# Four of sixteen first-norm transposes moved from TensorE to SBUF-to-SBUF transfers, with a new order of all tasks, in a gated convolution and mixer kernel

## The chip, the core and the metric

The kernel runs on one core of one Trainium2 chip. A core has five engines with queues of their own: TensorE (PE in the profile, with its weight loads as PEld), VectorE (DVE), ScalarE (ACT), GpSimd (POOL) and SyncE (SP), which here mainly issues transfers; sixteen DMA engines move the data. The metric is the device time of one execution in microseconds (us), lower is better.

## The reference, cut to what matters

There are 2048 tokens of 640 channels. Everything is bfloat16 at the borders.

```python
x = A_q
g = sigmoid((x * gate_w).sum(-1, keepdims=True))
# A: a 4-tap causal filter of k times v, then a convolution over all 2048 tokens, times q
kv = shift4(k, shift_k) * v
y  = irfft(rfft(pad(kv)) * rfft(pad(ssm_k)))[:2048] + kv * ssm_D
a  = x * y
# B: a mixer block on the same x
h  = gelu(layernorm(x) @ w1)                  # 640 -> 640
hs = concat(four quarters of h, shifted by +1, -1, +2, -2 tokens) @ w2
x1 = x + hs
b  = x1 + gelu(layernorm(x1) @ w3) @ w4       # 640 -> 1536 -> 640
out = g * a + (1 - g) * b
```

## The kernel before, in words

**Layout.** Token 16·p + s sits on partition p in slot s, so x is 16 slots of 128 tokens by 640 channels. A matmul that contracts over channels needs the normalised rows the other way round, channels on partitions; that turning is what the change is about.

**Branch B.** For each slot s, `st1.s` takes mean and variance (on DVE by batch-norm instructions, L577 to L581, or on ACT by two passes with an accumulator, L585 and L586), `rs1.s` makes the reciprocal root on POOL (L595), and `nm1.s` writes the normalised row into one of four `xn` buffers (DVE L631, ACT L601). For each pair of slots `tr1.s` turns both rows by 2 x 5 TensorE transposes of 128x128 into PSUM (L609), and `ev1.s` copies them into `xnT` (ACT L387 or DVE L389). `w1.G.part` (L689, and L693 for part 4) multiplies four slots of group G by w1; the token shifts are in the choice of slots that it reads, so group 3 with a shift of 2 reads slots 10 to 13. `g1` is the GELU (ACT L706), `w2.s` the second matmul (L715), `x1.s` the residual sum (DVE L722), `sq.s` the sum of squares (ACT L727). The second norm is done in the same way (`ve2`, `st2` on POOL, `nm2`), but its rows are turned by `dt2.s`, a transposing transfer from SBUF to SBUF that SP issues (L808), into `x1nT` or, for groups 1 and 3, into `XB`. `w3.c.fb` (L817) with `g2` (L824), and `w4.s` (L833, L842) follow.

**Branch A.** `ldsk` loads the filter; `trh` turns it on TensorE (L859), `evt` evicts it, `dfold` adds ssm_D on POOL (L865). `kv` is 32 passes on DVE (L878, L882, L886). The long convolution is a two-stage Fourier transform by matmuls: `s1h` (L911) and `s1x` (L913) with evictions `e1h` and `e1x` into the two `FS` buffers, `wF` to DRAM (L943), `rF` back (L957), `s2h` and `s2x` (L965), products `pa` and `pb` (DVE L980), `s3` (L993), `wG` (L1005), `rG` (L1019), `s4` (L1031). The end is `yq` (L1037), `ad` (L1064) or `ax` (L1045), `fo` (L1051) for the four last slots, and the stores `st`. `ldq` loads q again for `yq`.

**Order.** Each step is a task with a number; there are 778. `ORDER` is a list of these numbers, with a letter where a task that can run on several engines has its engine set. Each engine runs its own tasks in the order of the list, so a task that waits holds up all that stands behind it on that engine. `Plan.place` (L147) walks the list with a table of estimated durations and picks buffers by it: eight PSUM banks ("U", taken singly or as an aligned pair), four `xn`, two `FS` and so on. It also decides how many filler matmuls (L255) go in front of a TensorE task. Fillers are only put in until `w1.1.2` runs, which gives up the bank that they write. The 16 transposed rows of the first norm all go over TensorE, since the tuple that selects pairs for the transfers is empty:

```python
    DMA1 = ()
    pairs = [2, 4, 6, 8, 0, 14, 10, 12]
```

Of the kernel before, what the change touches and what calls it, by code (L numbers as in the profile page):

```python
# [42 lines left out]
163 406 130 128 156 157 440 105a 441a 407 159 153 154 106 160 461 47 445a 402 131 158 109a 155 442 111 132 137 443a
112a 408 161 462 466 48 138 409 463a 448 134 135 468 215p 216 449 164 140 469a 467a 119 413 141 51 221p 165 470 410 50
411 120a 166 222 223v 464 465a 167 474 471a 173 475a 174 171 217a 480 168 476 187 191 481a 482 193 477a 172 473 192
188 412 414 218 483a 478 169 195 189 170 181 415 416 417 479a 472 418 419 421 422 182 178 179 485 196 194 190 486 423
488 219a 484 225a 489a 175 220 487a 492 176 493a 136 203 424 204 494 425 490 206 498 207 495a 200 201 491a 420 426 427
428 430 502 499a 226 177 504 224 505a 211 503a 506 500 227 496 501a 239 507a 133 497 228 240 508 142 429 184 185 139
247 431 432 433 434 435 436 248 233 510 512 511a 231 513a 243 259p 509 249 514 235 234 260 232 244 515a 518 245 265p
250 236 229 52 519a 516 437 212 246 517a 520 241 242 237 230 522 266 261v 523v 526 238 530 527a 197 524 531a 528 255  # L50
521 529a 269v 262 525v 186 694v 263a 180 205 208 532 267v 303v 198 253 251 257 256 533 183 268 309v 353v 213 202 310
254 270 252 304 313a 264 307v 199 311v 534 535 537 271 539 258 536v 305a 538a 354 540 541v 272 571 566 542 555 293 544
543a 545 572 294 574 575a 289 567 569 570v 573a 550 290 277 598 556 558 278 568v 291 551 557a 292 552a 306 559v 553
546 554a 547a 279 280 283 576 577 284 548v 603 604 606 607a 599 587 287 635 312 273 600a 288 560 561 562 274 285 564a
605v 601 355v 308 286 563v 588 589a 590 591a 602v 582 275 276 578 314 614 580a 619 608 583 609 347p 348 579a 315 325
316 667 584v 549 585 357v 586a 214 615 617 335 616v 620 326 622 336 623a 592 618a 317 323 318 324 621v 593 610 611a
630 612v 333 636 334 631 633 329 349v 662 319 637v 624 634a 646 706 632a 625 594 281 330 320 647 595a 596v 648v 724
# [1049 lines left out]
```

## Time and profile before

| | us |
|---|---|
| device time, median of 3 runs (lowest, highest) | 225.08 (224.55, 225.7) |
| the profiled execution, its own time | 227.05 |
| its span, first to last instruction | 225.3 |
| TensorE busy (94%) | 212.7 |
| VectorE busy (84%) | 189.3 |
| ScalarE busy (69%) | 154.4 |
| GpSimd busy (20%) | 45.8 |

The profiled execution lies 1.75 us above its span and about 2 us above the median. In a row of a timeline the columns are start, duration, engine, line, operation, output and inputs, how many instructions are merged, and in brackets the idle time before with what ended it. In a row of grouped instructions they are line, engine, operation, count, then total busy time and mean duration in ns, then idle time before. In the table of stretches each row is a stretch of the span with its length, the busy time and count of each engine, the granted TensorE clock, the share of the DMA engines in use and their rate. "Median us to landing" is from issue to the last byte's arrival.

### The profile page before, as it was taken

The numbers are of one execution on the slowest core, as the hardware profiler recorded it, in microseconds if no ns is written. First come the engines' busy times: TensorE is split into PE (matmuls) and PEld (weight loads), VectorE is DVE, ScalarE is ACT, GpSimd is POOL, SyncE is SP. The second block draws the span as 40 slices with busy tenths as digits, with TensorE's granted clock in tenths as the row PEclk, the third lists the DMA queues.
The fourth block names the chain that finished last, engine by engine and source line by source line (L and its number), as shares of the span: only waits on it lengthen the run. The fifth ranks groups of instructions, "written<-read, shape, count | busy, mean of one in ns | idle before, by whom it ended". The sixth has DMA issues, their size and how long they took to land.

```text
span 225.3 us, 5381 instructions
## 1 busy us (share of the span) xinstructions
PE 212.7 (94%) x2161; PEld 106.4 (47%) x2178; DVE 189.3 (84%) x281; ACT 154.4 (69%) x225; POOL 45.8 (20%) x86
## 2 busy tenths in 40 slices
PE   3999889899999999999999999999999999999992
PEld 1576454466444444345543433334444555555561
DVE  7998896999999999997469989899857426989984
ACT  6998969799988999889658988888675002225000
POOL 7481532436200009930710000000000000000000
PEclk9999999999999999999999999999999999999999
DMA  6999999999999998979899989999992596988624
GB/s 193 281 308 232 220 237 238 327 233 327 349 240 287 241 272 252 379 270 270 193 367 311 373 154 285 316 304 309 247 255 88 185 374 209 281 250 249 203 64 116
DMA packets 39503, 57.94 MB, mean 257 GB/s; under 512 B 15027, under 2 KB 30645, under 8 KB 39478
## 3 DMA queue, kind: packets, MB, share of 16 engines
q1 hardware_dynamic: 39158, 57.27, 89.9%
q10 hardware_dynamic: 320, 0.33, 0.5%
q8 instruction: 17, 0.28, 0.5%
q14 instruction: 8, 0.07, 0.1%
HBM read 35.56 MB, written 18.36 MB: 239 GB/s over the span
## 4 chain that ended last, share of the span: by engine, by line
PE 63%; DMA 17%; DVE 12%; SPq 3%; issue 2%; ACT 1%; DVEq 0%
PE PS L817 18%; PE PS L833 17%; PE PS L715 9%; DMA x<-in_A_q_dram 7%; PE PS L965 5%; DMA W<-in_B_w_dram 4%; PE PS L689 4%; PE PS L993 4%; DMA SK<-in_A_ssm_k_dram 3%; DVE VC L878 3%; DVE VC L882 3%; DMA QO<-in_A_q_dram 2%; SPq L382 2%; PE PS L911 2%; PE PS L1031 1%
## 5 line engine op out<-in xcount | busy, mean ns | idle before, releaser
L824 ACT ACTIVATE h2T<-PS 128x512 bf16<-128x512 f32 x48 | 27.9, 605 | 27.3 <-PE PS L817 26.9
L833 PE MATMUL PS<-W,h2T 128*128 128x512 bf16 (+3 forms) x306 | 39.8, 298 | 0.3
L387 ACT CAST FS<-PS 128x1024 bf16<-128x1024 f32 x37 | 36.0, 1021 | 5.4 <-PE PS L913 3.5
L817 PEld LDWEIGHTS <-W 128*128 128x128 bf16 (+1 forms) x300 | 22.1, 103 | 29.4 <-issue 8.4
L833 PEld LDWEIGHTS <-h2T 128*128 128x128 bf16 (+1 forms) x312 | 22.4, 100 | 18.5 <-issue 1.6
L387 ACT CAST XH<-PS 128x1024 bf16<-128x1024 f32 x26 | 25.5, 1020 | 7.5 <-PE PS L965 7.4
L817 PE MATMUL PS<-x1nT,W 128*128 128x512 bf16 x120 | 28.5, 380 | 0.0
L817 PE MATMUL PS<-XB,W 128*64 128x512 bf16 (+1 forms) x180 | 28.5, 380 | 0.0
L980 DVE TENSOR_TENSOR PP<-XH 128x2048 bf16<-128x2048 bf16 x20 | 23.6, 1219 | 3.1 <-ACT XH L387 2.8
L878 DVE TENSOR_TENSOR VC<-K,VC 128x2560 bf16<-128x2560 bf16 x16 | 23.7, 1490 | 2.3 <-DMA W<-in_B_w_dram 2.1
L715 PE MATMUL PS<-W,hsT 128*128 128x128 bf16 (+1 forms) x155 | 23.5, 297 | 0.9 <-DMA W<-in_B_w_dram 0.6
L850 DVE TENSOR_TENSOR x<-PS,x 128x640 bf16<-128x640 f32 x12 | 9.8, 823 | 13.4 <-PE PS L833 13.2
L689 PE MATMUL PS<-xnT,W 128*128 128x512 bf16 x80 | 19.2, 379 | 0.1
L715 PEld LDWEIGHTS <-hsT 128*128 128x128 bf16 x160 | 12.8, 98 | 13.0 <-issue 1.1
L882 DVE TENSOR_TENSOR VC<-VC 128x2560 bf16<-128x2560 bf16 x12 | 17.9, 1489 | 0.3
L389 DVE CAST XH<-PS 128x1024 bf16<-128x1024 f32 x14 | 16.9, 1220 | 1.2 <-PE PS L965 1.1
L1037 DVE SCALAR_TENSOR_TENSOR W<-PS,GG,QO 128x640 bf16<-128x640 f32 x16 | 13.6, 877 | 2.4 <-PE PS L1031 1.9
L387 ACT CAST GS<-PS 128x1024 bf16<-128x1024 f32 x12 | 12.0, 1016 | 3.9 <-PE PS L993 3.9
L255 PE MATMUL PS<-C 128*128 128x512 bf16 x34 | 9.9, 434 | 3.8 <-DVE C L506 3.7
L842 PE MATMUL PS<-W,h2T 128*64 128x512 bf16 (+1 forms) x192 | 13.4, 299 | 0.0
L722 DVE SCALAR_TENSOR_TENSOR x<-PS,x 128x640 bf16<-128x640 f32 x16 | 12.8, 815 | 0.1
L965 PE MATMUL PS<-FX,TRIG 64*32 64x512 bf16 x320 | 12.4, 381 | 0.3 <-ACT GS L387 0.3
(115 smaller groups left out, 294.0 us busy)
## 6 DMA issues: line engine op xcount, KB each, us to landing
FH<-FS SPq DMA_DIRECT2D x8, 640.0 KB, 6.3
FXD<-FS SPq DMA_DIRECT2D x8, 640.0 KB, 5.0
FX<-FH SPq DMA_DIRECT2D x10, 512.0 KB, 6.0
FX<-FXD SPq DMA_DIRECT2D x10, 512.0 KB, 5.3
GX<-GD SPq DMA_DIRECT2D x8, 640.0 KB, 5.9
W<-in_B_w_dram SPq DMA_DIRECT2D x2, 1920.0 KB, 11.9
GD<-GS SPq DMA_DIRECT2D x8, 480.0 KB, 4.0
SK<-in_A_ssm_k_dram SPq DMA_DIRECT2D x5, 512.0 KB, 6.5
```

The source lines that it names most:

```text
L387: nc.scalar.copy(out=out, in_=in_)
L389: (nc.vector if t.on == "DVE" else nc.gpsimd).tensor_copy(out=out, in_=in_)
L689: nc.tensor.matmul(m[:, b, :], lhsT=W[:, 0, kb, 160 * fb:160 * fb + 128], rhs=rhs(kb, shifts[fb]), start=(kb == 0), stop=(kb == 4))
L715: nc.tensor.matmul(m[:, c0:c1], lhsT=env["hsT"][:, o.buf["hs"][0], fb, 128 * (s % 4):128 * (s % 4) + 128], rhs=env["W12"][:, 1, fb, c0:c1] ...
L817: nc.tensor.matmul(env.PS[q:q + w, t.buf["U"][0], :], lhsT=env["W3"][:, kb, 128 * fb + q:128 * fb + q + w], rhs=env.nT(int(nP[-1]))[:, :, ...
L824: nc.scalar.activation(out=env["h2T"][:, o.buf["h2"][0], fb, :], in_=env.PS[:, t.buf["U"][0], :], func=ACT.Gelu_apprx_tanh)
L833: nc.tensor.matmul(m[q:q + w, c0:c1], lhsT=env["h2T"][:, o.buf["h2"][0], fb, a:a + w], rhs=env["W4"][:, fb, c0:c1], start=(fb == 0), stop= ...
L878: nc.vector.tensor_tensor(out=VC[:, o], in0=env["K"][:, a + 3 - j:a + 7 - j, :], in1=w, op=ALU.mult)
L882: nc.vector.tensor_tensor(out=VC[:, 1], in0=VC[:, 1], in1=VC[:, 2], op=ALU.add)
L965: nc.tensor.matmul(env.U(t.buf["U"][0])[32 * j:32 * j + 32, gp, :], lhsT=CRI()[64 * gp:64 * gp + 64, 32 * pc:32 * pc + 32], rhs=X[64 * gp: ...
L980: nc.vector.tensor_tensor(out=env["PP"][:, o.buf["PP"][0], a, :].rearrange("p (b c) -> p b c", b=2), in0=X.unsqueeze(1).broadcast_to([P, 2 ...
L1037: nc.vector.scalar_tensor_tensor(out=u, in0=env.Uf(t.buf["U"][0])[:, 0:D], scalar=SS("GG")[:, s:s + 1], in1=env["QO"][:, 2 * q.buf["Q"][0] ...
```

## The change

The pairs (10, 11) and (12, 13) of the first norm leave TensorE. Their two `tr1` and two `ev1` tasks go, and four `dt1` tasks come, one per slot, each a transposing transfer from an `xn` buffer straight into `xnT`. Each holds its `xn` buffer until the transfer has landed. The estimates of `place` are altered in some places, it now models a hold-up of some DVE tasks beside two GpSimd tasks, the two readers of the PSUM of `tr1.0` and `tr1.14` are put in sequence by a new pool, and `ORDER` is a new list.

```diff
-    DMA1 = ()
+    DMA1 = (10, 12)
     pairs = [2, 4, 6, 8, 0, 14, 10, 12]
...
         if s0 in DMA1:
             for s, n in zip((s0, s0 + 1), nm):
                 dma(f"dt1.{s}", P * D * BF * 1.8, lambda t, s=s, n=n: nc.sync.dma_start_transpose(
                     out=env["xnT"][:, s + 2, :, :], in_=env["xn"][:, n.buf["xn"][0], :]), issue=1.25, use=[n], rel=[(n, "xn")],
                     w=[("xnT", s)], roles=("xnT",))
             continue
...
-        add(f"ev1.{s0}", {"ACT": 1.25, "DVE": 0.82}, 0, f_ev1, use=[tt], rel=[(tt, "U")], w=[("xnT", s0), ("xnT", s0 + 1)],
-            roles=("xnT",))
+        e1 = add(f"ev1.{s0}", {"ACT": 1.25, "DVE": 0.82}, 0, f_ev1, use=[tt], rel=[(tt, "U")], w=[("xnT", s0), ("xnT", s0 + 1)],
+                 roles=("xnT",), acq=(f"T{s0}",) if s0 in (14, 0) else ())
...
+            for o in (e1, eh):
+                o.rel.append((o, f"T{s0}", None))
...
+                if t.lock and e == "DVE" and held[0] <= at < held[1]:
+                    start[i] = at = held[1]
...
+                if t.hold and e == "POOL":
+                    held = (at, end[i])
```

The estimates altered are those of `ident`, `cjp`, `st1`, `nm1`, `evh`, `ve2`, `st2` and `dfold`. They change no instruction by themselves: they act through the buffers and fillers that `place` picks and through the search that made the list. Written out by name, the parts of the two lists that the prediction speaks of are these ("..." leaves tasks out):

```
PE before: fill gwm trh.1 sgm tr1.4 trh.2 trh.4 tr1.0 trh.3 tr1.2 tr1.14 w1.0.3 w1.0.0 w1.0.2 w1.0.1 trh.0 w1.1.2
  s1h.4 s1hr.4 tr1.6 s1h.0 w1.0.4 tr1.8 w1.1.0 s1h.7 s1h.6 s1h.5 w1.1.1 w1.1.4 s1hr.0 s1h.3 w1.1.3 w2.3 w2.1 s1h.1
  w2.2 w2.0 w2.4 s1h.2 tr1.10 w2.6 s1h.8 s1h.10 w2.5 s1h.11 w2.7 tr1.12 w1.2.2 s1hr.8 s1h.9 w1.2.0 s1h.12 ...
  w1.3.0 w2.10 w2.9 s1x.12 s1x.13 w2.8 ... gate s1xr.8 s1x.9 w3.0.0 ...
PE after:  fill gwm tr1.0 tr1.4 trh.0 tr1.2 w1.1.2 tr1.14 w1.0.3 trh.2 w1.0.0 w1.0.4 trh.1 w1.0.1 w1.0.2 tr1.8 trh.4
  sgm tr1.6 trh.3 w1.1.4 w1.1.1 s1h.4 s1h.7 s1h.5 s1hr.4 s1h.6 s1h.0 s1h.2 w1.1.0 s1hr.0 s1h.1 w1.1.3 s1h.3 w2.2 w2.0
  w2.3 w2.1 w2.5 s1h.12 w2.4 s1h.14 w2.6 s1hr.12 w2.7 s1h.13 w1.2.2 s1h.15 w1.3.2 w1.3.1 ... s1h.8 s1hr.8 s1h.9 w2.11
  s1h.11 w1.3.4 s1h.10 w1.3.3 s1x.12 s1x.14 w2.9 ... gate s1xr.8 s1x.10 w3.0.0 ...
SP before: ldsk1 ldx4 ldCJ ldgw ldx0 ldx14 ldx2 ldsk2 ldD ldsk4 ldsk3 ldw1 ldx6 ldsk0 bm ldx10 wCJ ldk15 ldk11 rCJ
  ldw2b3 ldw2a ldw2b1 ldw2b0 ldw2b2 ldkh1 wFh.4.0 wFh.4.1 ldk7 ldv3 ldk3 wFh.0.0 wFh.0.1 ldw3 ldkh0 ldv2 wFh.8.1 dt2.0
  wFh.8.0 wFh.12.1 wFh.12.0 dt2.1 ldv1 dt2.3 dt2.2 ...
SP after:  ldx0 ldx2 ldx4 ldgw ldx14 ldCJ ldx6 ldsk0 ldw1 ldsk2 ldx10 ldsk1 ldsk3 ldsk4 wCJ ldD ldk11 bm ldk15 rCJ
  ldw2a ldw2b0 ldw2b3 ldw2b2 ldw2b1 dt1.12 wFh.4.1 wFh.4.0 ldk7 ldv3 dt1.13 dt1.10 dt1.11 wFh.0.1 wFh.0.0 ldk3 ldv2
  dt2.0 wFh.12.0 wFh.12.1 ldw3 wFh.8.1 wFh.8.0 dt2.1 dt2.3 dt2.2 ldv1 ldkh0 ldkh1 ...
ACT before: warm abs sin0 sin1 sin st1.4 st1.0 st1.3 ev1.4 nm1.3 nm1.1 evt.1 evh.0 evt.3 ev1.14 st1.8 g1.0.2 g1.0.3
  g1.0.0 nm1.7 g1.1.2 g1.0.1 st1.11 e1h.0 e1hr.4 g1.0.4 e1h.7 e1h.6 e1h.5 g1.1.1 g1.1.0 e1hr.0 g1.1.4 g1.1.3 st1.10
  e1h.1 e1h.3 sq.1 nm1.10 ...
ACT after:  warm abs sin0 st1.0 st1.3 st1.4 st1.15 evh.0 st1.6 st1.9 st1.7 sin1 sin g1.1.2 g1.0.3 evt.2 nm1.8 st1.10
  g1.0.0 g1.0.4 g1.0.2 ev1.8 st1.13 nm1.10 g1.0.1 g1.1.4 g1.1.1 e1h.5 e1h.6 e1h.0 e1h.2 g1.1.0 e1h.1 g1.1.3 e1hr.0
  nm1.11 e1h.3 nm1.13 ... e1h.10 e1x.12 g1.3.3 e1x.14 nm2.1 ...
PE tail before: ... w4.13.0 w4.12.0 s4.12 s4.13 w4.13.1 w4.14.0 w4.12.1 w4.14.1 w4.15.0 w4.15.1
PE tail after:  ... w4.15.0 w4.14.0 s4.12 w4.14.1 w4.15.1 s4.13 w4.12.0 w4.13.0 w4.13.1 w4.12.1
DVE tail before: ... yq.13 ax.13 yq.12 ax.12 fo.12.0 fo.13.0 fo.12.1 fo.13.1 fo.14.0 fo.14.1 fo.15.0 fo.15.1
DVE tail after:  ... fo.14.0 fo.14.1 fo.15.0 fo.15.1 yq.12 yq.13 ax.13 ax.12 fo.12.0 fo.13.0 fo.13.1 fo.12.1
```

More of the change, by code (lines that the diff above doesn't have):

```diff
@@ L43 @@
[L43 to L57, printed above, removed]
@@ L102, in add @@
         t.kept = None
+        t.lock, t.hold = False, False
         t.acq = [(a, 1, a == "U") if isinstance(a, str) else a for a in acq]
@@ L116, in add @@
         return t
+    LOCKS = ("nm1.", "nm2.", "kv", "pa.", "pb.", "pc.", "ad.", "ax.", "phase1", "phand", "phsmall")
     def close(self):
+        for t in self.tasks:
+            t.lock, t.hold = t.name.startswith(self.LOCKS), t.name in ("cjp", "dfold")
         by_role = {}
@@ L621, in build @@
         for s in (s0, s0 + 1):
-            st1[s] = add(f"st1.{s}", {"DVE": 1.26, "ACT": 1.73}, 0, lambda t, s=s: f_st1(t, s), r=[("x", s, 0), ("x", s, 1)],
+            st1[s] = add(f"st1.{s}", {"DVE": 1.37, "ACT": 1.7}, 0, lambda t, s=s: f_st1(t, s), r=[("x", s, 0), ("x", s, 1)],
                          w=[("MV", s)])
@@ L632, in f_nm1 @@
                                             scalar2=SS("RS")[:, c], op0=ALU.add, op1=ALU.mult)
-            nm1[s] = add(f"nm1.{s}", {"DVE": 0.445, "ACT": 1.2}, 0, f_nm1, r=[("RS", s), ("x", s, 0), ("x", s, 1)],
+            nm1[s] = add(f"nm1.{s}", {"DVE": 0.445, "ACT": 0.95}, 0, f_nm1, r=[("RS", s), ("x", s, 0), ("x", s, 1)],
                          acq=("xn",))
@@ L661, in build @@
             a = -2 if s0 == 14 else 16
-            add(f"evh.{s0}", {"DVE": 1.0, "ACT": 1.3}, 0, f_evh, use=[tt], rel=[(tt, "U")], w=[("xnT", a), ("xnT", a + 1)],
-                roles=("xnT",))
+            eh = add(f"evh.{s0}", {"DVE": 0.9, "ACT": 1.3}, 0, f_evh, use=[tt], rel=[(tt, "U")], w=[("xnT", a), ("xnT", a + 1)],
+                     roles=("xnT",), acq=(f"T{s0}",))
+            for o in (e1, eh):
+                o.rel.append((o, f"T{s0}", None))
             add(f"evz.{s0}", {"POOL": 0.15, "DVE": 0.07}, 0, lambda t, z=(0, h0) if s0 == 14 else (127, h0):
```

23 lines of the change are left out of this document (8 added, 15 removed), and 5 rows, old and new, of the table ORDER.

## The prediction, made before the result

> **What bounds the kernel now.** I began with the table of stretches, cut where the chain of waits changes its character.
>
> ```profile
> 0.00:20.30 20.30, 16.13 (x144) 10.49 (x147) 18.33 (x59) 17.97 (x25) 12.64 (x33) 1.00 0.89 256
> 20.30:40.60 20.30, 17.58 (x143) 8.67 (x143) 16.22 (x39) 17.10 (x29) 6.13 (x11) 1.00 1.00 239
> 40.60:81.70 41.10, 40.81 (x323) 20.80 (x328) 40.28 (x50) 36.31 (x54) 9.54 (x17) 1.00 1.07 286
> 81.70:114.40 32.70, 32.37 (x207) 15.61 (x208) 26.35 (x38) 26.45 (x47) 17.49 (x25) 1.00 0.91 273
> 114.40:174.00 59.60, 59.01 (x832) 23.86 (x834) 51.96 (x50) 48.62 (x61) 0.00 (x0) 1.00 0.96 271
> 174.00:225.30 51.30, 46.76 (x518) 27.00 (x520) 36.14 (x47) 7.96 (x13) 0.00 (x0) 1.00 0.69 216
> ```
>
> From 40.6 to 174 us TensorE is idle for only 0.29 + 0.33 + 0.59 = 1.21 us. There the time is TensorE's work, and work taken out of that stretch comes off the end unless a new wait takes its place. Before 40.6 the picture differs: TensorE is idle for 4.17 + 2.72 us, and part of its busy time is filler.
>
> ```profile
> L255 PE MATMUL PS<-C 128*128 128x512 bf16 x34 | 9.9, 434 | 3.8 <-DVE C L506 3.7
> ```
>
> These 34 matmuls compute nothing. So 9.9 + 6.9 = 16.8 of the first 40.6 us hold no useful TensorE work. The chain of waits says why:
>
> ```profile
> 8.29 6.95 DMA SK<-in_A_ssm_k_dram
> 15.25 15.68 DMA x<-in_A_q_dram
> 30.95 9.63 DMA W<-in_B_w_dram
> ...
> 40.63 1.75 PE PS L715 x11
> ```
>
> The head is bound by loads, with the DMA engines in use for 0.89 and 1.00 of it, and ends when w2 lands, at 30.95 + 9.63 = 40.58 us. Only then can w2 start. A shorter head would need w2 earlier, or more other work ahead of it.
>
> **The change, part by part.** *Removed from TensorE:* tr1.10 and tr1.12.
>
> ```profile
> 48.45 0.56 PE PS L609 x10
> 54.38 0.56 PE PS L609 x10
> ```
>
> Both lie in the saturated stretch: 2 x 0.56 = **-1.12 us**, if nothing waits instead. Their evictions stood on ACT; ACT idles for 4.8 of the 41.1 us there, so I cost them at nothing.
>
> *Added on SP and the DMA engines:* four transposing transfers. The nearest rows are those of the second norm, the same shape.
>
> ```profile
> L808 SPq DMA_TRANSPOSE x1nT<-xn x8: 1206/1301/1937, 61.1 to 125.7; - x8
> DMA to landing us min/median/max: 2.7/5.3/7.0
> ```
>
> Four cost SP about 4 x 1.3 = 5.2 us; SP is not on the path there. The larger one for BT gives the same pace: it turns 16 blocks of 128x128, a row has 5, and 4.25 x 5/16 = 1.33 us.
>
> ```profile
> 157.89 4.25 SPq L1014 DMA_TRANSPOSE BT<-XB  x1
> ```
>
> I take 1.3 us of the DMA engines for each as well, an estimate from this pace. [...]
>
> *Head.* The same loads stand in front of w2 in both lists (all of x, all of SK, w1, two K blocks, bm, rCJ), so w2 should land at 40.6 again. w1 comes earlier, but w1's work done earlier only turns filler into waiting. What counts is the work done before the first w2 task: the new list has s1h.1 and s1h.2 there in addition, two of these:
>
> ```profile
> 43.52 0.43 PE PS L911 x2
> ```
>
> That is up to 2 x 0.43 = -0.87 us. Against it stands ACT, which must free the PSUM pairs. It gets nine st1 instead of six before the end of e1h.3, each the sum of these four:
>
> ```profile
> L585 ACT ACTIVATE JK<-x 128x640 bf16<-128x640 bf16 x6 | 4.5, 743 | 2.2 <-DMA x<-in_A_q_dram 2.1
> L585 ACT ACTIVATION_READ_ACCUMULATOR JK<-x 128x1 f32 x6 | 1.2, 199 | 0.0
> L586 ACT ACTIVATE JK<-x,SA 128x640 bf16<-128x640 bf16 x6 | 5.0, 828 | 0.2
> L586 ACT ACTIVATION_READ_ACCUMULATOR JK<-x,SA 128x1 f32 x6 | 1.1, 186 | 0.0
> L387 ACT COPY HT<-PS 128x2048 bf16<-128x2048 bf16 x2 | 3.7, 1855 | 0.0
> L387 ACT COPY xnT<-PS 128x1280 bf16<-128x1280 bf16 x2 | 2.5, 1226 | 1.1 <-DVE xnT L389 1.0
> L387 ACT CAST FS<-PS 128x1024 bf16<-128x1024 f32 x8 | 7.8, 1028 | 1.6 <-PE PS L911 1.6
> L601 ACT ACTIVATE xn<-x,NB,RS 128x640 bf16<-128x640 bf16 x4 | 3.6, 916 | 0.0
> ```
>
> So +3 x 1.96, less one evt (1.86), one ev1 (1.23), one e1h (1.03) and one nm1 (0.92): +0.8 us of ACT work, against 2.1 + 1.1 + 1.6 us of ACT waits shown there that may close. Following bank by bank, w2.2 needs the pair that e1h.1 frees, which I put at 41.4, within 40.6 to 42.5. That is +0.8, at best 0, at worst +1.9. One queue is moved past as well: wCJ on SP waits for cjp on POOL, which now stands behind rs1.9 and so behind the sixth st1 of ACT.
>
> ```profile
> 19.39 0.26 SPq L515 DMA_DIRECT2D CD<-VC  x1
> ```
>
> It goes out 3 us later by my count; SK and x, issued before it, keep the DMA engines busy meanwhile, and if they didn't, w2 would land up to 3 us later, part of B below. Head: -0.87 + 0.8 = **-0.1 us**, between -0.9 and +1.0.
>
> *w1.3.2*, the first reader of slots 10 to 13. Old TensorE had done the same work, and the 20 transposes, at this row:
>
> ```profile
> 56.74 1.24 PE PS L689 x5
> 43.98 1.93 ACT L387 CAST FS<-PS 128x1024 bf16<-128x1024 f32 x2 [1.58 <-PE PS L911]
> ```
>
> ```profile
> FH<-FS SPq DMA_DIRECT2D x8, 640.0 KB, 6.3
> ```
>
> It comes at 56.74 - 1.12 - 0.1 = 55.5. dt1.13 waits for nm1.13, which stands on ACT behind e1h.3; e1h.3 ended at 45.9 in the old list, so nm1.13 ends near 46, and dt1.13, dt1.10 and dt1.11 are issued at 46, 47.3 and 48.6. The last lands 5.3 to 7.0 us later: 53.9 to 55.6. The wait is 0 to 0.1, if the queue is as in those rows. Behind dt1.13 on SP wait wFh.0, ldk3, ldv2 and dt2.0. wFh.0 frees the FS buffer of s1h.8, which is needed 8 us after w1.3.2; landing in a median 6.3 us, it is in time. nm2.2 and nm2.0 on ACT need the xn buffers that dt1.12 and dt1.13 hold; these land first.
>
> *w3.0.0.* The second norm's last transposes:
>
> ```profile
> 69.76 1.72 ACT L601 ACTIVATE xn<-x,SB,r 128x640 bf16<-128x640 bf16 x2
> 74.39 2.57 SPq L808 DMA_TRANSPOSE x1nT<-xn  x2
> 81.74 2.33 PE L817 MATMUL PS<-x1nT,W 128*128 128x512 bf16 x10
> ```
>
> The last, dt2.2, was issued at 75.7 and w3.0.0 began at 81.74; 5.3 us of landing leave 0.7 of slack. In the new list w3.0.0 comes due at 81.74 - 1.12 - 0.1 = 80.5, while nm2.1 moves behind s1h.10's eviction and two of s1x, which I put at 73, then 3 x 1.3 of SP: dt2.2 issued at 75.8, landing at 81.1. The 5.3 us of added transposes on the DMA engines are mostly paid by ldv1 and ldkh moving behind (1.1 MB at 286 GB/s, 3.9 us). That is a wait of 0.6, of which I take **+0.5 us**, between 0 and +1.5.
>
> *40.6 to 174 otherwise.* The mix of w3, s2, s3, evictions and DVE products is reshuffled. No row shows the new mix; at most 1.2 us can be gained there, and the chance of small new waits is as large. I take 0, between -1.2 and +1.5.
>
> *Tail.*
>
> ```profile
> 212.84 8.03 PE L842 MATMUL PS<-W,h2T 128*64 128x128 bf16 x144
> 214.55 0.88 DVE L1037 SCALAR_TENSOR_TENSOR W<-PS,GG,QO 128x640 bf16<-128x640 f32 x1 [0.48 <-DMA QO<-in_A_q_dram]
> 218.16 3.76 DVE L1051 SCALAR_TENSOR_TENSOR QO<-PS,OG,W 128x512 bf16<-128x512 f32 x8
> L1051 DVE SCALAR_TENSOR_TENSOR QO<-PS,OG,W 128x128 bf16<-128x128 f32 x4 | 1.3, 341 | 0.0
> ```
>
> TensorE ends at 220.87, DVE at 221.92, 1.05 later, because yq.13 waited for its q and all eight fo pile up. The new list puts slots 14 and 15 first; after the last w4 only fo.12.1 is left, 0.34: **-0.7 us**, between -0.9 and 0 (ldq.12 late again).
>
> *Sum*, all durations being those of the one profiled execution: -1.12 - 0.1 + 0 + 0.5 + 0 - 0.7 = -1.4 us. Against the profiled execution that is 227.05 to 225.6 (span 225.3 to 223.9); on the median, 225.08 to **223.7 us**.
>
> **Rivals.** *A, the head gives all:* w2.2 at 40.6, no wait at w3.0.0, the 1.2 us of idle gone. -1.12 - 0.87 - 0.7 - 1.2 = -3.9, 221.2. For it: ACT's waits can close. Against: every term at its best.
>
> *B, the gain is eaten:* the transposes go from TensorE, but the place is taken by waits, at w2.2 (+1.9 in place of +0.8) and w3.0.0 (+1.0 in place of +0.5): +0.2, 225.3. It is also the case in which the change doesn't do what it says, TensorE losing 1.12 us of work and no time. For it: load and ACT set the head's end now.
>
> *C, slower: dt1.11 lands late at w1.3.2.* In the same stretch another transfer on the same queue landed far later:
>
> ```profile
> L561 SPq DMA_DIRECT2D K<-in_A_k_dram x1: 1373/1373/1373, 52.4 to 52.4; - x1
> DMA to landing us min/median/max: 13.0/13.0/13.0
> ```
>
> Ahead of dt1.13 stand wFh.4, ldk7 and ldv3, 2.6 MB, 9 us at 286 GB/s. From 48.6, a landing time above 55.5 + 1.4 - 48.6 = 8.3 us makes the change a loss; 10 us give 58.6, a wait of 3.1, and 225.08 - 1.4 + 3.1 = 226.8; 13.0 us give 229.8. Against it: that row stood behind the W3 load, which the new list moves back.
>
> *D, TensorE's clock.* The first fillers run slow, the later ones fast, in the same order of 128x512:
>
> ```profile
> 3.73 4.12 PE L255 MATMUL PS<-C 128*128 128x512 bf16 x11 [3.73 <-DVE C L506]
> 8.88 3.19 PE L255 MATMUL PS<-C 128*128 128x512 bf16 x14
> ```
>
> 0.375 against 0.228 us each: eleven cost 1.6 us more. Fillers end with w1.1.2, now seventh on TensorE and not seventeenth, so the waits of the head stay empty. Two slow starts would cost 3.2 us: 226.9. [...]
>
> **How the numbers follow.** Forecast 0.42, A 0.15, B 0.22, C 0.18, D 0.03. A measurement can tell about 0.5%, 1.1 us, from no change. The forecast's own range is 222.9 to 224.6; three quarters of its chance lie below 223.95. Faster: 0.32 + 0.15 = 0.47. Slower: C, D and 0.04 of B, 0.25. The rest, 0.28, is same. The range reaches from A's 221.2 to just above C at 10 us: 221.0 to 227.3.
>
> **What would show it.** Right: 20 fewer transposes, the first w2 between 40.6 and 42.5, w1.3.2 without a wait on xnT, w3.0.0 near 81, DVE ending 0.3 to 0.4 after TensorE. Wrong: TensorE idle on a transfer of xn into xnT (C), a granted clock below 1.00 after 17 us (D), or idle time in the stretch 114 to 174 well above 0.6 us, which I could not price.

## The result, and the profile after

The changed kernel took 228.02 us, the median of five runs (227.77 to 229.39), against 225.01 (224.55 to 225.7) for five runs of the kernel before: a ratio of 1.0143, 95% interval 1.0107 to 1.0178. It is slower by 3.0 us where 223.7 was forecast, and lies outside the range. Below, ratios are to runs of the kernel before on the same chip; they leave out disturbed runs, which the medians beside them include.

The profiled execution of the changed kernel took 228.0 us (span 225.9), like its other runs. The one of the kernel before that the prediction was worked out from took 227.05 (span 225.3), 2 us above its median. So the kernel before was profiled once more (run e1: 225.36 us, span 223.5), and the comparison goes by that profile. Its span and that of the changed kernel differ by 2.4 us, and it is these 2.4, not the whole 3.0, that the comparison can account for. First its table of stretches; the columns are as in the prediction.

```profile
20.30:40.60 20.30, 18.91 (x158) 9.71 (x158) 18.61 (x41) 18.46 (x31) 6.16 (x11) 1.00 1.01 261
40.60:81.70 41.10, 40.84 (x324) 20.66 (x327) 39.66 (x49) 36.71 (x53) 8.87 (x17) 1.00 1.08 287
81.70:98.00 16.30, 16.16 (x93) 6.83 (x94) 15.89 (x19) 14.61 (x25) 12.47 (x10) 1.00 0.84 273
98.00:114.40 16.40, 16.20 (x127) 8.68 (x128) 10.39 (x22) 11.13 (x22) 5.01 (x15) 1.00 0.98 267
114.40:174.00 59.60, 58.96 (x817) 23.96 (x819) 51.90 (x50) 48.95 (x62) 0.00 (x0) 1.00 0.97 272
```

The same stretches of the changed kernel:

```profile
20.30:40.60 20.30, 18.55 (x184) 11.01 (x183) 17.17 (x29) 19.07 (x29) 7.41 (x15) 1.00 1.02 254
40.60:81.70 41.10, 41.10 (x315) 20.17 (x314) 40.29 (x50) 37.72 (x58) 17.83 (x22) 1.00 1.06 279
81.70:98.00 16.30, 15.21 (x84) 6.26 (x83) 15.28 (x14) 12.69 (x21) 11.92 (x11) 1.00 1.05 339
98.00:114.40 16.40, 15.60 (x126) 8.71 (x133) 9.65 (x22) 11.71 (x20) 2.18 (x6) 1.00 0.89 256
114.40:174.00 59.60, 58.48 (x800) 23.22 (x800) 52.19 (x50) 48.81 (x62) 1.33 (x5) 1.00 0.86 265
```

From 40.6 to 81.7 TensorE of the changed kernel never idles. It then idles for 1.09, 0.80 and 1.12 us where it had idled for 0.14, 0.20 and 0.64. The last two columns show one more difference: from 81.7 to 98 the DMA engines go from a share of 0.84 to 1.05 and from 273 to 339 GB/s. Traffic that the kernel before had finished is still under way: up to 81.7 it has moved 22.3 MB, the changed kernel 21.5 (sums of rate times length).

TensorE's timeline names the places. The kernel before, second profile:

```profile
39.24 2.89 PE L715 MATMUL PS<-W,hsT 128*128 128x512 bf16 x19 [0.33 <-DMA W<-in_B_w_dram]
...
80.36 2.33 PE L817 MATMUL PS<-x1nT,W 128*128 128x512 bf16 x10
...
96.71 0.83 PE L913 MATMUL PS<-K,TRIG 64*128 64x512 bf16 x12
...
99.88 13.21 PE L833 MATMUL PS<-W,h2T 128*128 128x512 bf16 x95
...
113.02 0.62 PE L965 MATMUL PS<-FX,TRIG 64*32 64x512 bf16 x16
```

The changed kernel:

```profile
40.98 6.95 PE L699 MATMUL PS<-W,hsT 128*128 128x512 bf16 x50
...
55.10 5.13 PE L673 MATMUL PS<-xnT,W 128*128 128x512 bf16 x23
...
79.67 3.41 PE L801 MATMUL PS<-x1nT,W 128*128 128x512 bf16 x15
...
97.28 0.61 PE L897 MATMUL PS<-K,TRIG 64*128 64x512 bf16 x4 [0.98 <-DVE K L870]
...
100.46 13.20 PE L817 MATMUL PS<-W,h2T 128*128 128x512 bf16 x96
...
114.32 0.63 PE L949 MATMUL PS<-FX,TRIG 64*32 64x512 bf16 x16 [0.66 <-DMA FX<-FH]
...
151.51 0.84 PE L949 MATMUL PS<-FX,TRIG 64*32 64x512 bf16 x24 [0.93 <-DMA FX<-FXD]
```

| reached by TensorE | before, second profile | changed | difference |
|---|---|---|---|
| first w2 | 39.24 | 40.98 | +1.74 |
| w3.0.0 | 80.36 | 79.67 | -0.69 |
| first w4 | 99.88 | 100.46 | +0.58 |
| first read of FX (s2) | 113.02 | 114.32 | +1.30 |
| end of s3.9 | 172.63 | 175.10 | +2.47 |
| end of the span | 223.5 | 225.9 | +2.4 |

So the change starts w2 1.7 us late, is 0.7 us ahead at w3.0.0, and loses 3.2 us between there and s3.9; the tail is equal. The chain of waits of the changed kernel shows through what the lead goes:

```profile
78.88 6.17 DMA K<-in_A_k_dram
...
85.17 2.90 DVE VC L862 x2
...
100.46 3.43 PE PS L817 x24
...
103.92 0.84 DVE x L834
...
108.16 1.00 SPq L792
...
110.66 3.62 DMA FX<-FH
```

VectorE waits for the K halo rows, finishes its filter passes, TensorE's s1x.0 waits for these; then the second norm's transfers on SyncE's queue and a read of FX hold up s2. In the second profile of the kernel before, the chain is TensorE alone from 99.56 to 115 us.

### The profile page after: what moved, and what is told of

It is laid out like the page before. It is cut to its first block, busy times and chain, and to the rows that moved or that the text cites. A ratio compares the mean times of both kernels' runs of the same rounds, so it can differ in the third digit from the quotient of the medians.

```text
span 225.9 us, 5357 instructions
## 1 busy us (share of the span) xinstructions
PE 214.3 (95%) x2161; PEld 105.8 (47%) x2161; DVE 188.6 (83%) x264; ACT 156.0 (69%) x234; POOL 53.7 (24%) x93
## 4 chain that ended last, share of the span: by engine, by line
PE 52%; DMA 19%; DVE 18%; issue 4%; SPq 3%; ACT 2%; POOL 1%; DVEq 0%
PE PS L801 16%; PE PS L817 13%; DVE VC L862 7%; DMA SK<-in_A_ssm_k_dram 6%; PE PS L826 6%; DMA K<-in_A_k_dram 6%; PE PS L949 5%; DVE VC L866 4%; PE PS L699 4%; PE PS L977 4%; DMA FX<-FXD 3%; DMA x<-in_A_q_dram 2%; DVE x L706 2%; PE PS L1015 2%; DMA FX<-FH 2%
## 5 line engine op out<-in xcount | busy, mean ns | idle before, releaser
L808 ACT ACTIVATE h2T<-PS 128x512 bf16<-128x512 f32 x48 | 28.4, 605 | 25.8 <-PE PS L801 24.8
L817 PE MATMUL PS<-W,h2T 128*128 128x128 bf16 (+3 forms) x312 | 40.3, 299 | 0.1
L369 ACT CAST FS<-PS 128x1024 bf16<-128x1024 f32 x36 | 35.2, 1016 | 2.8 <-PE PS L897 2.0
L801 PE MATMUL PS<-XB,W 128*64 128x512 bf16 (+1 forms) x180 | 29.5, 380 | 0.0
L369 ACT CAST XH<-PS 128x1024 bf16<-128x1024 f32 x23 | 22.9, 1017 | 5.5 <-PE PS L949 5.5
L371 DVE CAST XH<-PS 128x1024 bf16<-128x1024 f32 x17 | 20.4, 1221 | 4.1 <-PE PS L949 3.1
L699 PE MATMUL PS<-W,hsT 128*128 128x512 bf16 (+1 forms) x160 | 23.4, 299 | 0.1
L369 ACT CAST GS<-PS 128x1024 bf16<-128x1024 f32 x14 | 13.8, 1016 | 6.6 <-PE PS L977 6.6
L711 ACT ACTIVATE JK<-x 128x640 bf16<-128x640 bf16 x16 | 11.8, 736 | 1.6 <-DVE x L706 1.4
```

The costliest lines, as they stand in the source:

```text
L369: nc.scalar.copy(out=out, in_=in_)
L371: (nc.vector if t.on == "DVE" else nc.gpsimd).tensor_copy(out=out, in_=in_)
L699: nc.tensor.matmul(m[:, c0:c1], lhsT=env["hsT"][:, o.buf["hs"][0], fb, 128 * (s % 4):128 * (s % 4) + 128], rhs=env["W12"][:, 1, fb, c0:c1] ...
L801: nc.tensor.matmul(env.PS[q:q + w, t.buf["U"][0], :], lhsT=env["W3"][:, kb, 128 * fb + q:128 * fb + q + w], rhs=env.nT(int(nP[-1]))[:, :, ...
L808: nc.scalar.activation(out=env["h2T"][:, o.buf["h2"][0], fb, :], in_=env.PS[:, t.buf["U"][0], :], func=ACT.Gelu_apprx_tanh)
L817: nc.tensor.matmul(m[q:q + w, c0:c1], lhsT=env["h2T"][:, o.buf["h2"][0], fb, a:a + w], rhs=env["W4"][:, fb, c0:c1], start=(fb == 0), stop= ...
```

## The experiments

The runs stand in five groups (e1 to e4, e5 to e8, e9 to e12, e13 to e16, e17 and e18), each on one chip beside runs of the kernel before. Differences in us are (ratio - 1) x 225.

### The two kernels again

e1 is the kernel before and e6 the changed one, without an edit.

> The kernel before, unchanged, for a second profile and the spans of its timed runs. Its first profiled execution took 227.05 us (span 225.3), 2.0 us above the median of its runs (225.01), while the changed kernel's profile stands at its own median (228.0). First theory: that one execution was an unlucky one (a late transfer somewhere): the new profile has a span of about 223 and shows which wait of the first is absent. Rival: profiling lengthens this kernel, whichever execution is looked at: span again 225 with the timed runs at 223. Times of the runs by either: 224.5 to 225.7.

Measured: 225.46 us, ratio 1.0009 (0.9976 to 1.0042), profile 225.36 with a span of 223.5. The first theory holds. The first profile has a wait that the second lacks:

```profile
25.42 1.21 PE L859 MATMUL PS<-ID,SK 128*128 128x128 bf16 x16 [0.60 <-DMA SK<-in_A_ssm_k_dram]
```

A block of SK came late in that one execution. So did w2, whose load stands like this in the chain of the second profile:

```profile
29.63 9.57 DMA W<-in_B_w_dram
```

It takes 9.6 us in both, but in the first profile SyncE issued it at 30.95, 1.3 us later, and from the first w2 on (40.63 against 39.24) TensorE is 1.4 us late. That the late SK made SyncE late is not shown. In five profiles with the old front and its 16 transposes the first w2 starts at 38.85 to 40.63; in eight of ten with the new front at 40.95 to 40.98, in the other two at 41.87 (e4) and 41.97 (e14).

> The changed kernel, unchanged, on the chip of the other runs: a second profile, to tell which of its waits are of the program and which of one execution. Expected by every theory: 227.8 to 228.4 us, and TensorE's waits at s1x.0 (0.98 us), at the first FX (0.66) and at the FX of 151.5 (0.93) there again, each within 0.3.

Measured: 228.70 us, 1.013 (1.0091 to 1.0168); the waits are there again with 0.94, 0.82 and 0.77 us. They belong to the program.

### Each half of the change by itself

```diff
 order before, DMA1 = (10, 12):
-tr1.12 ev1.12 ... tr1.10 ev1.10
+dt1.12 (behind nm1.12) ... dt1.13 (behind nm1.13) ... dt1.10 dt1.11 (behind nm1.10)
```

> The kernel before with the transfers alone: rows of slots 10 to 13 by four transposing transfers, put on SyncE's queue right behind their nm1 tasks; every other task where the order before has it. Theory 'order' (the loss is the new order's, not the transfers'): 224.0 to 225.3 us; TensorE is rid of 1.12 us and ScalarE of two evacuations before 56 us, but s1x.0 still starts at about 97.7 behind VectorE's chain, so most of it is not seen at the end. Rival 'transfers' (their packets or SyncE's 1.3 us each hold up what is behind them): 226.5 to 228 us.

```diff
 changed order, DMA1 = ():
-dt1.12 ... dt1.13 dt1.10 dt1.11
+w2.3 x1.3 tr1.12 ev1.12 ... w2.4 x1.5 tr1.10 ev1.10
```

> The changed kernel with the four transfers taken out and the two groups of ten transposes put back on TensorE (the first behind w2.3, the second behind w2.4's x1.5, both evacuated by ScalarE); the new order of all else kept. Theory 'order': 227.6 to 229.1 us, that is the 228.0 of the changed kernel plus 0 to 1.1 of TensorE. Rival 'transfers': 225 to 226.5 us, because the queue is rid of them.

Measured: transfers alone 228.94 us, 1.0125 (1.0074 to 1.0175), +2.8 us; order alone 230.36, 1.0214 (1.0176 to 1.0251), +4.8 us. My theory falls: the transfers alone cost as much as the whole change. In transfers alone two rows show where, one of VectorE and one of TensorE:

```profile
70.40 1.49 DVE L886 TENSOR_TENSOR K<-VC 128x2560 bf16<-128x2560 bf16 x1 [4.42 <-DMA VC<-in_A_v_dram]
...
62.60 0.59 PE L911 MATMUL PS<-HT,C 128*128 128x512 bf16 x2 [2.85 <-ACT FS L387]
```

VectorE stands 4.42 us for the V rows of kv2. TensorE stands 2.85 us behind an eviction into FS, before which ScalarE stood 4.14 us, and 1.49 us more at 75.61 behind VectorE; w3.0.0 comes at 84.92. Order alone is also the result of where I put the transposes back (TensorE waits 1.35 us for PSUM at 48.02 behind the first), so it says only that the new order is no gain with the transposes at these two places.

### What the transfers do in the old order

```diff
-nc.sync.dma_start_transpose(out=env["xnT"][:, s + 2, :, :], in_=env["xn"][:, n.buf["xn"][0], :])
+nc.sync.dma_start(out=env["xnT"][:, s + 2, :, :],
+                  in_=env["xn"][:, n.buf["xn"][0], :].rearrange("p (c t) -> p c t", c=5))
```

> The run of transfers alone with plain copies in place of the four transposing transfers (rows of slots 10 to 13 left untransposed, so what follows from them is not the reference's). Theory 'engine time of transposing': the V rows of kv2 land 3 to 4 us earlier than 70.3, VectorE's wait of 4.42 falls to 1 or less: 225 to 226.3 us. Rival 'SyncE' (what holds the rows up is the queue's own time: 1.25 us for each issue and 4.2 us behind nm1.10): 228 to 229.

Measured: 1.0063 (1.0029 to 1.0096), +1.4 us (median 227.67, runs from 225.43 to 229.85). VectorE's wait is halved, TensorE's 2.85 us fall to 0.59, and the truth lies between the two theories:

```profile
67.07 1.49 DVE L886 TENSOR_TENSOR K<-VC 128x2560 bf16<-128x2560 bf16 x1 [2.33 <-DMA VC<-in_A_v_dram]
```

By the middle values half of the harm is the transposing and half the place, but the two intervals overlap, so that split is not shown. What the transposing takes is in the DMA view of 50 to 70 us, in 40 slices of 0.5 us (busy tenths, then GB/s). Transfers alone:

```profile
DMA  9999009997897899999999999995999999997999
GB/s 236 178 183 41 4 10 199 349 328 164 164 328 164 154 358 385 384 399 381 379 417 389 424 412 399 332 264 227 418 425 413 306 230 284 256 277 192 294 248 330
```

The same with plain copies:

```profile
DMA  8958999999999999999999999999999999923999
GB/s 166 143 136 266 230 328 402 384 395 392 359 353 392 400 432 399 399 393 399 399 415 410 215 199 291 207 198 236 197 259 307 401 338 227 106 26 69 415 366 379
```

Around dt1.10 and dt1.11, issued from 47.12 to 49.65, the engines first move next to nothing for 1.5 us, although K rows were put in the queue at 49.70, and then only 154 to 349 GB/s for 4 us. From 40 to 60 us they move 5.08 MB with the transposing and 6.12 MB with plain copies; at the latter's 306 GB/s the difference is 3.4 us of the sixteen engines, an estimate from this one pair of profiles.

```diff
 e7, on SyncE's queue of transfers alone:
-ldw3 ldkh0 ldv2
+ldv2 ldw3 ldkh0
```

> The kernel before with the transfers, as in the run of transfers alone, and one more edit: W3's load and the read ldkh0 go behind the V rows of kv2 (ldv2) on SyncE's queue. In transfers alone VectorE stood 4.42 us for those V rows (from 65.97 to 70.40) and everything after it was 4.56 us late. Theory 'FIR chain': the rows land 5 to 6 us earlier, the wait goes, and VectorE's chain ends where it does in the kernel before (96.4 us): 224.6 to 225.8 us, no gain from the 1.12 us that TensorE is rid of, since s1x.0 starts at the end of that chain (96.71) either way. Rival 'TensorE': its 1.12 us show at the end, 223.7 to 224.5. Rival 'engine time': the wait goes to another transfer, 226.5 to 228.5.

Measured: 227.22 us, 1.0066 (1.0033 to 1.0098), +1.5 us. By the middle values that is half of the harm gone; the intervals of e3 and e7 overlap a little. VectorE's wait is gone, and ScalarE's, which stood in transfers alone too, is still there, here put down to a write that frees an FS buffer:

```profile
60.80 1.01 ACT L387 CAST FS<-PS 128x1024 bf16<-128x1024 f32 x1 [3.94 <-DMA FH<-FS]
```

TensorE stands 2.65 us behind it at 61.87, where it stood 2.85 before. So the next edit puts those writes first as well.

```diff
 e17, on SyncE's queue of e7, and nm1.10 ahead of sq.1 on ScalarE:
-dt1.10 dt1.11 ldk3 wFh.0.0 wFh.0.1
+ldk3 wFh.0.0 wFh.0.1 dt1.10 dt1.11
```

> The order before with all four transfers, W3 and ldkh0 behind the V rows of kv2 as in e7 (227.22 us), and now the K rows ldk3 and the writes wFh.0.0 and wFh.0.1 ahead of dt1.10 and dt1.11 (nm1.10 goes ahead of sq.1 on ScalarE). In e7 ScalarE stood 3.94 us for a write of FH and TensorE 2.65 us behind it. Theory 'engine time' (the four transfers hold the queue for about 5 us in all, the second pair for 2.5; whoever is behind waits): the wait at 61.9 falls below 0.5, but the rows of slots 10 and 11 land at 58 or later and TensorE waits 0.5 to 2 us for them at w1.3.2: 225.5 to 227.0 us. Rival 'place' (it was the place of the FH writes alone): 224.0 to 225.2, level with the kernel before or ahead of it.

Measured: 230.23 us, 1.020 (1.0152 to 1.0249), +4.5 us, worse than either theory. Now the transposed rows themselves are late:

```profile
58.81 2.32 PE L689 MATMUL PS<-xnT,W 128*128 128x512 bf16 x5 [3.51 <-DMA xnT<-xn]
```

The wait at 61.87 is gone, and the one that has come is the one that rival C feared. In this row five 128x512 matmuls take 2.32 us, 1.24 in the old profile: the granted clock behind the wait is 0.59 and 0.55 (last section).

```diff
 e18, order before:
-DMA1 = ()
+DMA1 = (12,)
-tr1.12 ev1.12
+dt1.12 (behind nm1.12) ... dt1.13 (behind nm1.13)
```

> The kernel before with one pair of slots by transfer (12 and 13, on SyncE's queue behind their nm1 tasks, as in transfers alone), the other pair by TensorE, all else where it was. With both pairs the time was 228.94 us, 3.4 to 3.7 over the kernel before. Theory 'engine time' (cost by the transfer): half of that, 226.5 to 227.5 us, with VectorE's wait for the V rows of kv2 at 1.5 to 2.5 us instead of 4.42. Rival 'SyncE's stop behind nm1.10' (the 4.2 us for which the queue stood there): 225.0 to 226.0, the loss is the other pair's.

Measured: 225.66 us, 1.0011 (0.9974 to 1.0049), no difference that can be told. VectorE's wait for the V rows is 0.53 us. One pair early costs nothing and gains nothing; the harm of transfers alone comes with the second pair, which SyncE issues at 47.12 in transfers alone, 8.6 us behind dt1.13, in front of K rows, V rows and the writes of FH. That half the transfers cost half is refuted. Without the second pair SyncE also loses its stop of 4.2 us behind nm1.10: the K rows go out at 44.02, in transfers alone at 49.70. e18 doesn't tell that stop from the pair's own transfers; e8, which keeps the stop and not the transposing, has +1.4.

### Where in the new order the time goes: grafts

Four kernels take one order up to a task and the other from there on.

```diff
 e9:  changed up to the first w4, then before
 e10: before up to the first w4, then changed
 e11: changed up to the first w3.3, then before
 e12: before up to the first w3.3, then changed
```

> Graft: the changed kernel's order (with the four transfers) up to its first w4 (about 100 us), then every task that is left in the order of the kernel before. Theory 'middle' (the transfers and the new front cost no more than the 0.6 us by which the first w4 is late, 100.46 against 99.88; the rest is lost by the new order between there and s3.9, the second norm's transfers and the reads of FX and FXD): 225.5 to 226.4 us. Rival 'front' (the traffic put off by the transfers is owed past 100 us and no order behind it can mend that): 227.3 to 228.6.

> The reverse graft: the order before, with its transposes on TensorE, up to its first w4 (about 100 us), then the changed kernel's order. Theory 'middle': 226.8 to 228 us, the loss is there without any of the four transfers. Rival 'front': 224.8 to 225.8.

> The changed kernel's order up to its first w3.3 (about 186 us), then the order before. From the end of s3.9 to the end of the span the kernel before took 50.9 us in its second profile (172.63 to 223.5) and the changed one 50.8 (175.10 to 225.9). Theory 'no tail' (the tails are worth the same; what the first profile of before showed as 0.75 us at the end was that one execution's): 227.8 to 229.0 us. Rival (the new tail is worth the 0.7 that was forecast): 229.0 to 229.8.

> The order before up to its first w3.3, then the changed kernel's order. Theory 'no tail': 225.0 to 226.0 us, as before. Rival (the new tail is worth the 0.7 that was forecast): 224.4 to 224.9, faster than both kernels.

| | median us | ratio (95%) | us |
|---|---|---|---|
| e9, new front, old rest | 226.93 | 1.0083 (1.0059 to 1.0107) | +1.9 |
| e10, old front, new rest | 226.82 | 1.0078 (1.0048 to 1.0107) | +1.8 |
| e11, new front and middle, old tail | 227.57 | 1.0106 (1.0079 to 1.0133) | +2.4 |
| e12, old front and middle, new tail | 229.95 | 1.0202 (1.0157 to 1.0247) | +4.5 |

Both parts cost: the new front, with the transfers, 1.9 us, and the new rest, with none of the four in it, 1.8. Together that is more than the 3.0 of the whole change, so the two do not simply add. Neither "middle" nor "front" alone is right. In e10 TensorE waits at the reads of FX and GX where the kernel before has no such wait:

```profile
113.20 0.63 PE L965 MATMUL PS<-FX,TRIG 64*32 64x512 bf16 x16 [0.23 <-DMA FX<-FH]
...
144.94 0.41 PE L965 MATMUL PS<-FX,TRIG 64*32 64x512 bf16 x8 [0.43 <-DMA FX<-FXD]
...
200.20 1.01 PE L1031 MATMUL PS<-GX,BT 128*64 128x512 bf16 x12 [0.31 <-DMA GX<-GD]
...
207.67 0.73 PE L1031 MATMUL PS<-GX,BT 128*64 128x512 bf16 x8 [0.67 <-DMA GX<-GD]
```

They add up to 1.64 us; this profile's span is 2.3 us longer than that of the kernel before (225.8 against 223.5). In e9 the read of FX is late although everything behind the first w4 is the old order, so part of the front's cost falls due later:

```profile
114.73 0.63 PE L976 MATMUL PS<-FX,TRIG 64*32 64x512 bf16 x16 [0.96 <-DMA FX<-FH]
```

By this row e9 is 1.71 us behind the kernel before (113.02), and its span is 1.7 longer (225.2): all that it loses is lost by here.

e11 and the changed kernel can't be told apart by their intervals, so the new tail is worth nothing that was measured. Behind the old middle it is a heavy loss. The profile of e12 shows one read as its largest piece, but it is of the slowest execution (232.52 us), so how much of the +4.5 that read makes is not shown:

```profile
209.55 1.28 PE L1031 MATMUL PS<-GX,BT 128*64 128x512 bf16 x8 [3.18 <-DMA GX<-GD]
```

### The waits of the new order, one by one

```diff
 e2, SyncE's queue of the changed kernel:
 ldk3 ldv2
+ldkh0 ldkh1
 dt2.0 wFh.12.0 ... wFh.8.0 dt2.1 dt2.3 dt2.2 ldv1
-ldkh0 ldkh1
```

> The changed kernel with one edit in its order: the reads of the K halo rows (ldkh0, ldkh1) go from behind dt2.2 and ldv1 (issued at 77.8 to 78.9 us) to just behind ldv2. Theory 'order': VectorE's FIR chain (all kv tasks, busy without a gap from 40 to 98 us) is what the lead of 2.1 us at w3.0.0 ran into, so without its wait of 0.78 us at 85.17 kv0.v ends 0.8 earlier, at 96.3, and s1x.0 starts 0.6 to 0.9 earlier: 227.2 to 227.8 us if half or more of it lasts to the end. Rival 'DMA engines full': the rows only change places in the queue (89% of the span busy) and something else comes later: 228.0, within 0.4, with a new wait of the same size.

Measured: 229.73 us, 1.0178 (1.0134 to 1.0222). VectorE's wait for the halo went, but ScalarE then waited 1.61 us for a write of FH and TensorE behind it, and w3.0.0 came at 81.00 in place of 79.67.

```diff
 e13, the same queue:
 wFh.8.1 wFh.8.0
+ldkh0 ldkh1
 dt2.1 dt2.3 dt2.2 ldv1
-ldkh0 ldkh1
```

> The changed kernel with the reads of the K halo rows (ldkh0, ldkh1) put between wFh.8.0 and dt2.1, where SyncE's queue stands for 2.3 us anyway (70.3 to 72.7 us), instead of behind dt2.2 and ldv1. Theory 'place': the rows land at about 78, VectorE's wait of 0.74 to 0.78 us for them goes, TensorE's wait at s1x.0 falls from 0.94-0.98 to 0.3 or less, and dt2.2 still lands in time for w3.0.0: 227.3 to 228.2 us. Rival 'queue full' (as in the earlier placing at 57 us, which cost 1 us): dt2.1 to dt2.2 come 1.5 us later and w3.0.0 waits for them: 228.2 to 229.2.

Measured: 228.62 us, 1.0157 (1.0122 to 1.0193). The halo's wait went again, and the V rows' came, on VectorE:

```profile
83.67 1.49 DVE L897 TENSOR_TENSOR K<-VC 128x2560 bf16<-128x2560 bf16 x1 [0.82 <-DMA VC<-in_A_v_dram]
```

and TensorE, which reached w3.0.0 at 79.65 without a wait, stood behind ScalarE right after it:

```profile
81.62 2.32 PE L828 MATMUL PS<-x1nT,W 128*128 128x512 bf16 x10 [0.71 <-ACT FS L396]
```

"Queue full" had the time right, though it put the wait at w3.0.0 itself.

> The changed kernel with its four transposing transfers replaced by plain copies of the same rows (same source, same 160 KB, same place in xnT, same spot on SyncE's queue): the rows of slots 10 to 13 are left untransposed, so what is computed from them is not the reference's. Theory 'engine time of transposing': from 40.6 to 60 us the DMA engines move 259 GB/s at a share of 1.06 with the transfers and 308 at 1.04 without, which makes an estimate of 1.45 us of all sixteen engines for one transfer of 160 KB where plain traffic at 296 GB/s takes 0.55; with plain copies the queue is 3.6 us shorter, K and V rows and halos land earlier, VectorE's FIR chain loses its waits: 225.5 to 227.2 us. Rival 'order' (what is lost lies in the places of the tasks): 228.0, within 0.4.

The edit is that of e8, made in the changed kernel (e5). Measured: 229.68 us, 1.0186 (1.0141 to 1.0231); the forecast gain of 1 to 2.5 us didn't come. The engines are freed, but nothing uses them. A stretch of the plain copies:

```profile
56.00:60.00 4.00, 4.00 (x20) 1.81 (x19) 3.96 (x4) 3.99 (x7) 3.70 (x3) 1.00 0.87 202
```

and of the changed kernel (e6):

```profile
56.00:60.00 4.00, 4.00 (x21) 1.81 (x19) 3.96 (x4) 3.99 (x7) 3.83 (x3) 1.00 1.08 288
```

The share falls from 1.08 to 0.87, because SyncE issues nothing between 56.5 and 58.70, and then stands from 62.8 to 68.92 behind wFh.8.1, as it does in the changed kernel (56.6 to 58.83, 62.7 to 69.05). The order that was made for the transfers can't use what they leave.

```diff
 e14 (changed kernel) and e15 (kernel before), kv2.m1 and kv2.a1 only:
-lambda t, j=j, a=a: tap(t, j, 1 if j == 3 else 2, a)
+(lambda t: None)
-acc
+(lambda t: None)
```

> The changed kernel with two of VectorE's FIR tasks left out (kv2.m1 and kv2.a1, 1.53 us each; the second tap of slots 8 to 11 is not added, so what follows from them is not the reference's). Theory 'FIR chain' (the lead of TensorE is lost because s1x.0, and behind it the second norm with its transfers, stand at the end of VectorE's chain): the chain ends up to 3 us earlier, TensorE's wait at s1x.0 goes and the first FX is reached 1.5 us earlier or more: 226.0 to 227.0 us. Rival 'owed traffic' (reads and writes come no earlier, whatever VectorE does): 227.7 to 228.7.

> The kernel before with the same two FIR tasks left out. In its second profile TensorE comes to s1x.0 at 96.71 us without a wait, 0.3 behind the chain's end (96.41): TensorE and VectorE's chain are tied. Theory 'tied': without 3 us of the chain TensorE is alone, and the time stays within 0.5 of 225.4. Rival 'the chain sets the kernel before': 223 to 224.5 us.

Measured: e14 229.51 us, 1.0181 (1.014 to 1.0222); e15 225.23, 0.9994 (0.9961 to 1.0026). The theory that VectorE's filter is what the lead runs into falls. With 3 us less of it VectorE waits instead, in e14 mostly for TensorE's w2 and then for loads

```profile
67.20 0.82 DVE L706 SCALAR_TENSOR_TENSOR x<-PS,x 128x640 bf16<-128x640 f32 x1 [2.30 <-PE PS L699]
...
84.46 1.49 DVE L870 TENSOR_TENSOR K<-VC 128x2560 bf16<-128x2560 bf16 x1 [0.21 <-DMA VC<-in_A_v_dram]
86.53 2.89 DVE L862 TENSOR_TENSOR VC<-K,VC 128x2560 bf16<-128x2560 bf16 x2 [0.57 <-DMA K<-in_A_k_dram]
```

and in e15 for loads

```profile
65.26 1.49 DVE L886 TENSOR_TENSOR K<-VC 128x2560 bf16<-128x2560 bf16 x1 [2.86 <-DMA VC<-in_A_v_dram]
```

TensorE's wait at s1x.0 of e14 is 0.94 us as before; s1x.0 itself came at 98.64, 1.4 later, of which 1.0 was there at the first w2 (41.97, two waits for SK). So in the kernel before VectorE's filter does not set the time by itself: with less of it the loads take its place, as far as one profile shows. That VectorE, TensorE and the DMA queue are nearly tied there fits these runs; it is not shown by itself.

```diff
 e16, e11 with the halo reads as in e13, and:
-x1.12 ... st2.4 nm2.4
+st2.4 nm2.4 x1.12
-s2x.7.0 s2x.7.1 ... w3.2.8 g2.2.8
+w3.2.8 g2.2.8 s2x.7.0 s2x.7.1
```

> The changed kernel with the order before from the first w3.3 on (227.57 us by itself) and three places mended: the halo reads as in e13; st2.4 and nm2.4 ahead of x1.12 on VectorE, so that the second norm's first transfer starts 0.8 us earlier; w3.2.8 ahead of s2x.7, to cover TensorE's wait for FX at 151.5. If each wait costs what it shows (0.9 at s1x.0, 0.7 to 0.8 at the first FX, 0.2 to 0.9 at 151.5): 225.3 to 226.4 us. Rival (each mended wait comes back behind another): 227.2 to 227.9.

Measured: 228.32 us, 1.0134 (1.0108 to 1.0159), against e11's 1.0106. The first FX came at 113.85 without a wait, 0.8 us earlier than in e11, and the wait at 151.51 grew to 1.39 us, where e11 waits 0.24 at 151.16, for VectorE:

```profile
151.51 0.84 PE L976 MATMUL PS<-FX,TRIG 64*32 64x512 bf16 x24 [1.39 <-DMA FX<-FXD]
```

Both reach that row within 0.4 us of each other. The rival's mechanism holds, a mended wait comes back behind another, though the time is above its 227.2 to 227.9.

## Why the prediction was wrong, step by step

- **TensorE -1.12: right.** From the first w2 to w3.0.0 the kernel before takes 41.12 us and the changed one 38.69, 2.43 less. Of this 0.87 are s1h.1 and s1h.2, done ahead of w2, and 0.39 is one s1x that now follows w3.0.0 (an s1x takes 0.39 in the second profile of before). That leaves 1.17.
- **Head -0.1: the start was right, in part by luck, and the base wrong.** The first w2 came at 40.98, within the forecast 40.6 to 42.5, with TensorE busy and not waiting. The sum of ScalarE's work behind it took off one nm1 too many (both lists have three before e1h.3), so by its own prices it was +1.8 and not +0.8, and w2 still came 0.4 earlier than forecast. The base, 40.63, was that execution's late w2; its repeat gives 39.24. Against that the head costs 1.74 - 0.87 = +0.87. I knew that the profile lay 2 us above the median, and carried its sum over to the median as if the 2 us lay evenly; 1.4 of them lay in the head of the kernel before, so the term was too small by 1 us.
- **w1.3.2 without a wait: right.** TensorE runs from 55.10 on without one. **w3.0.0, a wait of 0.5:** it was 0, and the start 79.67, against the 81 forecast.
- **40.6 to 174 otherwise 0: the step that failed.** After w3.0.0 the changed kernel loses 3.2 us; less the s1x that moved there, the term put at 0 measured +2.8. TensorE's waits at s1x.0 (0.98), at the first FX (0.66) and at 151.51 (0.93) are 2.57 us, the rest lies in smaller pieces. I had named idle time there as what would make the prediction wrong, bounded it at 1.5, and left the transfers' 5.3 us on the DMA engines "mostly paid" by ldv1 and ldkh moving behind. These did move behind, and became a wait: the halo rows at 85.17 are ldkh. It is not the whole cause, since taking that wait away gave no time back (e2, e13).
- **Tail -0.7: nothing of it.** From TensorE's end to the end of the span the first profile of before has 4.4 us, the second 3.8, the changed kernel 3.7. VectorE ends 0.39 us after TensorE in the changed kernel, as forecast, but also in the second profile of before: the gap I meant to remove was mostly that execution's.

Of the rivals, B came nearest by mechanism (TensorE loses the work and no time) but had too few waits in it. C has the measured time between its two prices, 226.8 and 229.8, but that is luck: its wait at w1.3.2 was not there. It showed in e17. A fall of the granted clock, as D has it, showed behind long waits in e7, e12 (0.50 in both) and e17 (0.55), not through the fillers. The slow first fillers that D was worked out from ran at a granted clock of 1.00 in the first profile of before (3.73 to 7.85 us), so what made them slow is not shown.

Shown: the transfers in the old order cost 2.8 us (e3), nothing with one pair (e18), and 1.4 as plain copies (e8); the new front costs 1.9 us and the new rest 1.8 (e9, e10); four edits that took waits away in the crowded stretch brought other waits and no gain (e2, e13, e16, e17). Argued, not shown: that traffic put off by the transfers is what makes the new front late; e5 speaks against the transposing as such there. The new rest waits at reads of FX and GX (e10). Open: which of its placings makes these reads late, since mending one of them (e16) only moved the wait.

## What to carry to other kernels

Where TensorE, VectorE and the DMA queue are all nearly full, taking work from one and giving it to another can be a loss even if the first gets faster, as here (+2.8 us in e3): price the added transfer by what stands behind it in the queue, not by the engine that issues it. Before a sum is made from one profile, ask whether that execution is typical; if it lies above the median, find the row where it is late. And put an early transfer where the queue has nothing urgent behind it, as the one pair of e18 that cost nothing.
